# Three small transfers of each head pair's normalisation issued by GpSimd instead of SyncE

## The chip, the cores and the metric

The kernel runs on one core of a Trainium2 chip. The metric is device time in microseconds (us), the median of several runs; lower is better. The engines are PE (TensorE, with PEld for its weight loads), DVE (VectorE), ACT (ScalarE), POOL (GpSimd) and SP (SyncE, which here only issues transfers). Each engine works through its own list of instructions in order.

## What is computed

Attention over 4 batches, 12 heads, 448 positions and a head size of 64, and behind it two feed-forward blocks on 1792 tokens (768 to 2048 to 768, the activation is the square of a relu). All data are float32.

```python
scores = scale * np.matmul(q, k.transpose(0, 1, 3, 2))
scores = cap * np.tanh(scores / cap)
scores = scores - np.max(scores, axis=-1, keepdims=True)
attn = np.exp(scores)
attn = attn / (np.sum(attn, axis=-1, keepdims=True) + 1e-09)
x = np.matmul(attn, v)          # then heads side by side: 1792 x 768
x = (np.maximum(x @ w_in, 0) ** 2) @ w_out      # first block
x = (np.maximum(x @ w_in, 0) ** 2) @ w_out      # second block
```

## The kernel before

Heads are taken two at a time, so a batch has 6 pairs and the kernel has 24. Attention of batch 0 runs first, beside the decoding of weights (`w_early`, `dec`, lines 185 to 211). Then `mlp(b)` (line 246) does the first feed-forward block of batch b on PE, and `weave` (line 711) mixes the attention of batch b+1 into it, piece by piece. The second block (`mlp2`, line 368) comes behind. Each float32 product is made of three matmuls on split operands (`mm`, line 235).

One pair is the generator `att_pair` (line 570): scores and tanh (lines 584 to 594), exp and the product with v (lines 627 to 643), and the normalisation (lines 644 to 690), which this study is about. The normalisation of a pair is a chain of steps, each waiting for the one before:

- The row sums of exp come either out of the matmul itself (pairs called native, line 654 copies them to partition 0 of `sb`) or from two POOL instructions (`partition_all_reduce`, line 610, 10 pairs). They are 2 x 448 numbers on one partition.
- Line 668: a transfer spreads them over 128 partitions (`comp`, 128 x 7). Lines 674 and 675: DVE adds eps and takes the reciprocal.
- Line 676: a transfer writes the 896 numbers to memory (`row`).
- Line 678: two transfers, one for each head, read them back and lay each row over 64 partitions (`rec`, 128 x 448).
- Line 687: DVE multiplies the unnormalised result `u` by `rec`; lines 688 and 689 (ACT, DVE) split it into the two parts of `x`, the input of `mlp(b)`.

The last pair of batch 0 has no such chain, so 23 pairs have one, with four transfers each. Besides these, SP issues every load and store of the kernel: raw weights (line 175, 768 KB each), decoded weights out and in (lines 203 and 183), q, k, v, and results. The order of the instructions on every engine is not the order of the source: the tile framework plans it with a model of the timing (`schedule_with_timeline_sim=True`, line 824), and puts in the semaphore waits. `behind()` (line 147) ties a step's DVE, ACT or SP instructions behind the weight work recorded so far.

Of the kernel before, what the change touches and what calls it, by code (L numbers as in the profile page):

```python
# [17 lines left out]
B, H, S, D = 4, 12, 448, 64  # L18
# [84 lines left out]
def program(ctx: ExitStack, tc, work, capv, sct, eps, qT, kT, v, v1, vl, w_in, w_out, out, guard):  # L103
    nc = tc.nc
# [41 lines left out]
    @contextmanager  # L146
    def behind():

        now, n = dict(marks), len(nc.cur_bb.bb.instructions)
        yield  # L150
        for ins in nc.cur_bb.bb.instructions[n:]:
            if ins.engine in now:
                tc.add_manual_dep(ins, now[ins.engine], mybir.DependencyInfo(
                    mybir.DependencyClass.NoSync, mybir.DependencyReason.DATA), reason="behind the weights")
# [415 lines left out]
    def att_pair(b, pr):  # L570
# [24 lines left out]
        half = [slice(j * D, (j + 1) * D) for j in range(2)]  # L595
        s, sb = work
# [50 lines left out]
        rec = a1.tile([P, S], F32, tag="rec", name="rec")  # L647
        for j in range(2):
# [8 lines left out]
            else:  # L657
                o = a1.tile([P, S], F32, tag="rest", name="rest")
                ACT.activation(o[main], pv[rest], AF.Copy)
                DVE.tensor_tensor(u[main], pv[main], o[main], op=ALU.add)  # L660
        if last:
            DVE.reciprocal(rec, rec)
        else:

            w = 2 * S // P
            comp = a2.tile([P, LINE // 4], F32, tag="comp", name="comp")[:, :w]
            row = dram2.tile([2, S], F32, tag="row", name="row")
            nc.sync.dma_start(out=comp, in_=sb[:1].rearrange("o j s -> o (j s)"))
            yield
            wait = b > 0 and pr < NP - 1  # L670
            if wait:
                yield
            with behind() if wait else ExitStack():
                DVE.tensor_scalar(comp, comp, eps, None, op0=ALU.add)
                DVE.reciprocal(comp, comp)
                nc.sync.dma_start(out=row.rearrange("j s -> (j s)").rearrange("(p w) -> p w", w=w), in_=comp)
                for j in range(2):
                    nc.sync.dma_start(out=rec[half[j]], in_=row[j:j + 1].to_broadcast([D, S]))
            yield
            if wait:  # L680
                yield
                yield
# [9 lines left out]
    def attention(b):  # L692

        live = []
        n = 0
        pr = 0
        while pr < NP or live:
            if pr < NP and n % (LAG0 if b == 0 else LAG) == 0:
                live.append(att_pair(b, pr))
                pr += 1  # L700
            n += 1
            for gen in list(live):
                if next(gen, "end") == "end":
                    live.remove(gen)
            yield
# [125 lines left out]
```

## Time and profile before

| | |
|---|---|
| median of 3 runs | 1117.32 us (1116.66 to 1118.54) |
| the profiled run | 1120.3 us |
| span of its instructions | 1118.5 us |
| PE busy | 1088.4 us (97%) |
| DVE, ACT busy | 865.7 us (77%), 742.3 us (66%) |
| POOL busy | 63.1 us (6%), 24 instructions |
| granted PE clock, mean | 0.993 |

The span reaches from the first to the last instruction; 1.8 us of the profiled run lie around it, and the profiled run is 3.0 us above the median. Times below are microseconds from the start of the span. A busy PE is not PE at its peak, since matmuls are pipelined and their ends are modelled. "Releaser" is what a trace view names as the event that ended a wait; where the named instruction had long been done, another was the real one.

### The profile page before, as it was taken

Reading aid. Unit: us, or ns where it says so; the run is one execution under the profiler, and the core shown is the slowest. Engines: PE = TensorE matmul, PEld = TensorE weight load, DVE = VectorE, ACT = ScalarE, POOL = GpSimd, SP = SyncE. Lnnn points to the kernel's source line nnn. Section 1 sums busy time; section 2 is a strip of 40 time slices with the busy share of each in tenths; the row PEclk is TensorE's granted clock in tenths of the full one; section 3 lists DMA queues with packets and bytes.
Section 4 is the critical chain, followed back from the end, with each engine's and each line's share of the span. In section 5 each row is a group of like instructions: output and inputs, shape, how many; then the busy total and the mean of one; then the engine's idle time right before and its main releaser. Section 6 shows DMA issues by size and latency. Waiting matters only on the chain.

```text
span 1118.5 us, 14514 instructions
## 1 busy us (share of the span) xinstructions
PE 1088.4 (97%) x5088; PEld 948.9 (85%) x5088; DVE 865.7 (77%) x1148; ACT 742.3 (66%) x1036; POOL 63.1 (6%) x24
## 2 busy tenths in 40 slices
PE   6988999989999999999999999999999999999998
PEld 4555989879888799799899999999998999999997
DVE  7778889786989778899778876797789846657663
ACT  6997987657796759998747843565755535555542
POOL 0000002020222021022020000000000000000000
PEclk9998999999999999999999999999999999999999
DMA  8886776855846575756477886885345543333441
GB/s 337 280 297 209 239 241 204 281 160 163 267 139 208 162 258 183 234 189 205 125 246 272 300 291 210 291 301 160 118 134 157 158 136 113 100 112 101 136 126 67
DMA packets 92177, 221.11 MB, mean 198 GB/s; under 512 B 16576, under 2 KB 43072, under 8 KB 92096
## 3 DMA queue, kind: packets, MB, share of 16 engines
q1 hardware_dynamic: 92096, 220.10, 60.2%
q8 instruction: 42, 0.69, 0.2%
q14 instruction: 39, 0.32, 0.1%
HBM read 174.28 MB, written 45.70 MB: 197 GB/s over the span
## 4 chain that ended last, share of the span: by engine, by line
PE 71%; DVE 5%; DMA 4%; ACT 2%; issue 1%; SPq 0%; DVEq 0%; ACTq 0%
PE ps L241 29%; PE st L409 18%; PE st L487 16%; PE pv L641 4%; PE sc L588 3%; DMA rec<-row 1%; DMA scr<-wf 1%; DVE wlo L218 1%; DMA comp<-work 1%; DMA row<-comp 1%; DMA work<-y 0%; DVE wf L194 0%; DVE pl L636 0%; DVE r L193 0%; DVE u L687 0%
## 5 line engine op out<-in xcount | busy, mean ns | idle before, releaser
L218 DVE TENSOR_TENSOR wlo<-wf,whi 128x768 fp32r<-128x768 f32 x240 | 236.9, 989 | 62.6 <-ACT whi L217 62.1
L217 ACT ACTIVATE whi<-wf 128x768 fp32r<-128x768 f32 x240 | 201.1, 839 | 100.0 <-PE st L409 48.4
L241 PE MATMUL ps<-x,whi 128*128 128x448 f32 x768 | 220.6, 368 | 0.0
L241 PE MATMUL ps<-g,whi 128*128 128x448 f32 x768 | 219.9, 367 | 0.0
L409 PE MATMUL st<-xx,whi 128*128 128x448 f32 x672 | 190.9, 367 | 0.0
L487 PE MATMUL st<-t,whi 128*128 128x448 f32 x672 | 187.1, 367 | 0.0
L241 PEld LDWEIGHTS ps<-x,whi 128*128 128x128 f32 x768 | 144.7, 188 | 14.2 <-issue 2.2
L241 PEld LDWEIGHTS ps<-g,whi 128*128 128x128 f32 x768 | 144.4, 188 | 13.7 <-issue 1.8
L241 PE MATMUL ps<-x,wlo 128*128 128x448 f32 x384 | 142.5, 373 | 3.3 <-ACT x L688 3.1
L241 PE MATMUL ps<-g,wlo 128*128 128x448 f32 x384 | 142.1, 371 | 0.0
L487 PEld LDWEIGHTS st<-t,whi 128*128 128x128 f32 x672 | 126.2, 188 | 11.9
L409 PEld LDWEIGHTS st<-xx,whi 128*128 128x128 f32 x672 | 126.2, 188 | 11.3
L409 PE MATMUL st<-xx,wlo 128*128 128x448 f32 x336 | 122.2, 367 | 0.0
L487 PE MATMUL st<-t,wlo 128*128 128x448 f32 x336 | 117.8, 367 | 0.4 <-ACT xx L342 0.4
L593 ACT ACTIVATE t<-sc,sct 128x896 f32<-128x896 f32 x96 | 86.4, 914 | 13.3 <-PE sc L588 12.7
L588 PE MATMUL sc<-ql,kk 128*128 128x448 f32 x192 | 79.9, 416 | 14.1 <-DVE kk L552 8.1
L610 POOL PARTITION_ALL_REDUCE work<-work x20 | 62.9, 3194 | 503.6 <-DVE work L604 293.8
L628 ACT ACTIVATE t<-t,capv 128x896 f32<-128x896 f32 x96 | 89.5, 950 | 0.4
L342 ACT ACTIVATE t<-g 128x896 fp32r<-128x896 f32 x48 | 45.4, 950 | 66.7 <-PE st L487 65.7
L241 PEld LDWEIGHTS ps<-x,wlo 128*128 128x128 f32 x384 | 72.1, 188 | 11.8 <-ACT x L688 4.0
L343 DVE TENSOR_TENSOR t<-g,t 128x896 fp32r<-128x896 f32 x48 | 52.0, 1088 | 37.4 <-ACT t L342 37.4
L241 PEld LDWEIGHTS ps<-g,wlo 128*128 128x128 f32 x384 | 72.1, 188 | 7.5 <-issue 1.6
(102 smaller groups left out, 1508.7 us busy)
## 6 DMA issues: line engine op xcount, KB each, us to landing
wf<-scr SPq DMA_DIRECT2D x215, 384.0 KB, 3.2
raw<-w_in SPq DMA_DIRECT2D x32, 768.0 KB, 5.7
raw<-w_out SPq DMA_DIRECT2D x32, 768.0 KB, 5.9
scr<-wf SPq DMA_DIRECT2D x32, 384.0 KB, 5.4
scr<-wa SPq DMA_DIRECT2D x64, 192.0 KB, 4.3
scr<-ss SPq DMA_DIRECT2D x48, 192.0 KB, 4.2
q_r<-qT SPq DMA_DIRECT2D x18, 448.0 KB, 4.6
k_r<-kT SPq DMA_DIRECT2D x18, 448.0 KB, 4.0
```

The source lines that it names most:

```text
L217: mark(ACT.activation(hi, f, AF.Copy))
L218: mark(DVE.tensor_tensor(lo, f, f32(hi), op=ALU.subtract))
L241: PE.matmul(ps, lhsT=w[:, i, :], rhs=x[part][:, j, :], start=first and n == 0, stop=last and n == len(terms) - 1)
L342: ACT.activation(hi, t, AF.Copy)
L343: DVE.tensor_tensor(lo, t, f32(hi), op=ALU.subtract)
L409: PE.matmul(ps, lhsT=w[:, i + c, :], rhs=x[:, kk_, c, :], start=first and c == 0 and n == 0, stop=c == 2 and n == 2, skip_group_check=not ...
L487: PE.matmul(banks[b][e], lhsT=w[:, 3 * f + e, :], rhs=x[:, f, :], start=first and q == f == n == 0, stop=q == 3 and f == 1 and n == 2, ski ...
L588: PE.matmul(sc[:, 0 if shared else j, :S], lhsT=kchunk(kk, j, c), rhs=q[:, j, :], start=n == 0 if shared else n % 2 == 0, stop=n == 3 if s ...
L593: ACT.activation(t[c], sc[:, 0, :S] if shared else sc[:, :, :S], AF.Tanh, scale=sct)
L610: POOL.partition_all_reduce(out[:, j], s[:, j], P, op)
L628: ACT.activation(t[c], t[c], AF.Exp, scale=capv)
L641: PE.matmul(pvs[j], lhsT=vv[:, j, c, :], rhs=m_ if c == KC else m_[:, j, :], start=c == 0 and m_ is moving[0], stop=c == KC and m_ is movi ...
```

## The change

All four transfers of the chain move from SP's list to POOL's. What they move, and what waits for them, stays as it was.

```diff
-            nc.sync.dma_start(out=comp, in_=sb[:1].rearrange("o j s -> o (j s)"))
+            nc.gpsimd.dma_start(out=comp, in_=sb[:1].rearrange("o j s -> o (j s)"))
...
-                nc.sync.dma_start(out=row.rearrange("j s -> (j s)").rearrange("(p w) -> p w", w=w), in_=comp)
+                nc.gpsimd.dma_start(out=row.rearrange("j s -> (j s)").rearrange("(p w) -> p w", w=w), in_=comp)
                 for j in range(2):
-                    nc.sync.dma_start(out=rec[half[j]], in_=row[j:j + 1].to_broadcast([D, S]))
+                    nc.gpsimd.dma_start(out=rec[half[j]], in_=row[j:j + 1].to_broadcast([D, S]))
```

## Rows read from the trace of the kernel before

**Rows 1.** The page, part 1: engine, busy us (share), instructions.

```profile
PE 1088.4 (97%) x5088; PEld 948.9 (85%) x5088; DVE 865.7 (77%) x1148; ACT 742.3 (66%) x1036; POOL 63.1 (6%) x24
```

**Rows 2.** Windows: stretch, length, busy us (count) by engine, PE clock, DMA share, GB/s.

```profile
56.00:84.00 28.00, 22.82 (x78) 14.15 (x76) 21.82 (x36) 26.81 (x36) 0.00 (x0) 0.94 0.90 296
84.00:100.00 16.00, 11.96 (x38) 7.79 (x38) 15.81 (x20) 10.60 (x15) 0.00 (x0) 0.79 0.65 220
```

**Rows 3.** Timeline of PE, 56 to 92: start, us, instruction [idle before, releaser].

```profile
83.44 0.68 PE L241 MATMUL ps<-x,wlo 128*128 128x448 f32 x2 [3.14 <-ACT x L688]
88.15 0.71 PE L588 MATMUL sc<-ql,kk 128*128 128x448 f32 x1 [4.04 <-DVE ql L553]
```

**Rows 4.** Waits of DVE, 28 to 100: us in total, times, longest us.

```profile
DVE u L687 <- DMA rec<-row: 4.8, 3, 3.0
```

**Rows 5.** Timeline of DVE, 28 to 112.

```profile
82.15 0.62 DVE L687 TENSOR_TENSOR u<-u,rec 128x448 f32<-128x448 f32 x1 [3.03 <-DMA rec<-row]
```

**Rows 6.** Issue to landing of lines 668, 676, 678, in that order, 28 to 100.

```profile
DMA to landing us min/median/max: 4.4/6.1/8.2
...
DMA to landing us min/median/max: 4.0/4.7/6.7
...
DMA to landing us min/median/max: 2.7/3.3/6.0
```

**Rows 7.** The same three landings for pair 3 of batch 0 alone, 62 to 77.

```profile
DMA to landing us min/median/max: 5.5/5.5/5.5
...
DMA to landing us min/median/max: 6.1/6.1/6.1
...
DMA to landing us min/median/max: 5.7/5.8/6.0
```

**Rows 8.** The same lines, 100 to 600: SP's issue (ns min/median/max), then landing.

```profile
L668 SPq DMA_DIRECT2D comp<-work x18: 497/501/1112, 101.3 to 569.7; - x18
DMA to landing us min/median/max: 2.1/3.3/6.1
...
L676 SPq DMA_DIRECT2D row<-comp x18: 319/320/424, 124.2 to 572.6; - x18
DMA to landing us min/median/max: 1.4/2.6/6.6
...
L678 SPq DMA_DIRECT2D rec<-row x36: 450/532/1601, 127.2 to 576.5; - x36
DMA to landing us min/median/max: 2.7/3.0/7.1
```

**Rows 9.** Lines 610 and 194, all their instructions: ns min/median/max, first and last.

```profile
L610 POOL PARTITION_ALL_REDUCE work<-work x20: 2951/3246/3318, 173.2 to 564.0; - x20
...
L194 DVE SCALAR_TENSOR_TENSOR wf<-wf,r x32: 919/957/2600, 19.7 to 235.9; 128x768 int32<-128x768 int32 x32
```

**Rows 10.** Waits of PE, whole span.

```profile
PE pv L641 <- DVE pl L636: 4.6, 3, 3.0
```

**Rows 11.** Waits of SP's list, whole span.

```profile
SPq L678 <- DMA row<-comp: 48.1, 23, 4.7
```

**Rows 12.** Chain that ended last, 240 to 262: start, us, what.

```profile
251.38 6.95 DMA rec<-row
```

**Rows 13.** Timeline at the ends of attention of batches 1, 2 and 3.

```profile
259.11 0.58 ACT L688 ACTIVATE x<-u 128x448 fp32r<-128x448 f32 x1 [6.27 <-DVE u L687]
...
259.74 0.47 PE L241 MATMUL ps<-x,wlo 128*128 128x448 f32 x1
...
421.99 0.58 ACT L688 ACTIVATE x<-u 128x448 fp32r<-128x448 f32 x1 [4.95 <-DVE u L687]
...
423.29 0.36 PE L241 MATMUL ps<-x,wlo 128*128 128x448 f32 x1
...
580.30 0.58 ACT L688 ACTIVATE x<-u 128x448 fp32r<-128x448 f32 x1 [4.36 <-DVE u L687]
...
585.23 0.36 PE L241 MATMUL ps<-x,wlo 128*128 128x448 f32 x1
```

## Prediction

> **What bounds the kernel now.** The page comes first: PE is busy for 1088.4 of 1118.5 us [rows 1], so 30 us at most can be won by feeding PE better, whatever is done to transfers. The second view is the table of windows, which says where PE is not full. Between 56 and 100 us, the end of batch 0's attention, PE idles 9.2 us (28 - 22.82 and 16 - 11.96), and its granted clock falls to 0.94 and 0.79, that is, part of the stretch at the lower of its two levels [rows 2]. The third view, PE's timeline, gives the two largest gaps: 3.14 and 4.04 us [rows 3]. The first names ACT's step on x, which stands behind the product with `rec`. In the second half of that stretch DVE is busy 15.81 of 16 us [rows 2]: there DVE sets the pace, and PE's gaps are DVE's delays. The fourth view, DVE's waits, shows what delays it: 4.8 us for `rec`, three times [rows 4], 3.03 us of it in one wait that ends at 82.15 [rows 5]. So in batch 0 the normalisation chain stands on the path, and there alone by much. Later PE is nearly full, and the chain touches the end at one point per batch: the last pair's x, which `mlp(b)` needs for its sixth chunk.
>
> **What is moved.** 23 pairs x 4 transfers = 92 issues leave SP and come to POOL, which has 20 instructions in the program proper [rows 9]. Nothing is added and nothing computed differently. The waits go along: SP stood 48.1 us, 23 times, for `row` to land before it could issue line 678 [rows 11]; now POOL stands there.
>
> *SP relieved.* What was queued behind SP's 48.1 us are loads and stores of weights. The waits that stand out on DVE in batch 0 and on PE later are for `rec` and `pl` [rows 4, 10], not for weights, so I count this at nothing; if that cover were gone, the bound is 2.1 us (48.1 / 23) for each load that was late.
>
> *POOL's queue.* Behind a POOL transfer waits the next pair's all-reduce, and behind the two all-reduces of a pair (2 x 3.25 = 6.5 us [rows 9]) waits an earlier pair's transfer if the planner orders it so. A chain would then be 6.5 us later; behind batch 0 PE's longest waits are for `pl` and not for x [rows 10], so outside the three stage ends I take nothing.
>
> *Issue on POOL.* No POOL issue stands in the trace. Bounds: SP's own for the same transfers, 0.50 + 0.32 + 0.53 + 0.53 = 1.9 us per chain [rows 8], and POOL's one kind of real work, 3.25 us an instruction [rows 9], so 13.0 us per chain. It can't be below SP's by more than that 1.9 us. I take 1.0 us an issue, twice SP's row, because the transfers are the same and an all-reduce reads and writes whole tiles: 4.0 us a chain, +2.1 us. The Trainium skill (DMA: Bandwidth & Descriptors, SWDGE vs HWDGE vs iDMA) says that GpSimd makes the descriptors in software and is slower to the first byte, about 1 us against 0.6; by that the sum would be +0.4 us on each of three hops, and no run here shows it yet.
>
> *Queueing.* On SP a transfer of 3.5 KB stands behind 768 KB weight loads issued just before it. The medians from issue to landing in batch 0 are 6.1, 4.7 and 3.3 us, 14.1 together [rows 6]; the smallest seen later are 2.1, 1.4 and 2.7, 6.2 together [rows 8]. So about 8 us of a chain in batch 0 is queueing; pair 3, the one behind the 3.03 us wait, took 5.5, 6.1 and 5.8 [rows 7], 17.4 us, or 11.2 over the smallest. A list of POOL's own may pass all of SP's backlog or none of it. I take half, because the same DMA engines are 0.90 busy in that stretch [rows 2]: -5.6 us for pair 3, and with the dearer issue -5.6 + 2.1 = -3.5 us.
>
> Here a page speaks for and against. The Trainium skill (DMA: Bandwidth & Descriptors, Queues, rings and completion order) says that an engine goes round between the queues that have work, packet by packet, by which nearly the whole -11.2 us would come. The same page (Issuing engines are not separate DMA queues) says that transfers issued by several engines run on the same 16 and that only issue time is saved, by which nothing of it would come: that is the second rival below.
>
> *Batch 0.* 3.5 us earlier covers the 3.03 us wait; the two smaller ones would go too, 4.8 us in all [rows 4]. Only what is not absorbed by a later DVE wait counts. Behind the 3.03 us DVE runs full (15.81 of 16 [rows 2]), so that one counts whole: -3.0 us, between 0 (the next wait, for loads, takes it) and -4.8.
>
> *Later batches.* Medians are 3.3 + 2.6 + 3.0 = 8.9 us against 6.2 [rows 8]; half of 2.7 is -1.3, with issue +2.1 it is +0.8 us a chain, hidden wherever x is early. At the three stage ends the room is: batch 1, 259.11 + 0.58 = 259.69 against PE's 259.74, 0.05 us; batch 2, 422.57 against 423.29, 0.7 us; batch 3, 580.88 against 585.23, 4.35 us [rows 13]. In batch 1 the last hop took 6.95 us [rows 12], 4.25 over the smallest; half of that, 2.1, pays the dearer issue. I take 0 for all three, with +0.8 at batches 1 and 2 (+0.9 together beyond the room) as the near bound and the first rival as the far one.
>
> *DVE beside POOL.* Beside an all-reduce a DVE instruction of 0.96 us took up to 2.60 [rows 9], and PE lost 4.6 us in three gaps to that kind of delay [rows 10]: 0.23 us per all-reduce. If an issue hurt DVE in proportion to its length, 92 x 0.23 x 1.0 / 3.25 = 6.5 us. It can't be a gain, since POOL only gets more work. I take 0, because a transfer's issue does not read tiles, and keep +6.5 as the bound. The Trainium skill (SBUF — State Buffer, Who interferes with whom) has the clash the other way round too: DVE instructions that take both ports lock GpSimd out, and descriptors wait; by the 0.96 us of a DVE instruction here [rows 9] that would be under 1 us an issue.
>
> *The plan.* The order of all engines is planned with modelled times, so 92 moved issues can shift neighbours. The price of such a shift is that of the single gaps that such delays leave now, 0.5 to 3 us [rows 10], either way.
>
> **Sum.** Against the profiled run, 1120.3 us: -3.0 + 0 + 0 = 1117.3 us; that run was 3.0 above the median, so the median comes to 1114.3 us.
>
> **The rivals**, all on the median, 1117.3 us.
>
> 1. *Longer hops show at the stage ends (slower).* Place: PE's sixth chunk at 259.7 and 423.3. Price of an issue i: the chain grows by 4i - 1.9 - 2.1 there, and batch 0's gain is 5.6 + 1.9 - 4i = 7.5 - 4i while it is under 3.0. Loss (beyond 0.05 and 0.7 us of room) and gain meet at i = 1.4 us; from there on it is slower. At i = 2.0 the chain grows 4.0: 3.95 + 3.3 = 7.25 us of gaps and nothing gained in batch 0. Gaps of that size now (3.14 + 4.04) go with a clock of 0.79 over 16 us [rows 2, 3], another 3.4 us: 1117.3 + 10.6 = 1127.9 us. For it: all-reduces of 3.25 us show POOL's software as slow. Against: the work per issue is small. Chance 0.14.
> 2. *The queue is not left behind (slower, less).* The backlog sits in the shared DMA engines, and the chain only gets +2.1 us of issue: the 3.03 us wait grows by 2.1, batch 1 loses 2.05, batch 2 1.4, together +5.6: 1122.9 us. For it: the engines are 0.90 busy in batch 0 and 0.65 behind it [rows 2]. Against: line 676 moves the same 3.5 KB in 1.4 to 6.7 us [rows 6, 8] with what SP issued just before. Chance 0.14. The Trainium skill's second sentence above is this rival.
> 3. *Hidden anyway (no change).* The 3.03 us reappear as a wait for a load or for ACT, which is busy 26.81 of 28 us from 56 to 84 [rows 2]; or the gain is paid back at batches 1 and 2. 1117.3 us. Chance 0.28.
>
> **How the numbers follow.** The forecast, 1114.3 us, has 0.44. A measurement of this kernel tells about 0.2% (2.2 us) from no change; faster by more is below 1115.1. The range goes from 1110.5 (-4.8 instead of -3.0, and 2 us of the plan) to 1124.0, which takes in the second rival and the DVE bound beside the gain (-3.0 + 6.5) and leaves the far rival out. Chances: faster 0.44, same 0.28, slower 0.28.
>
> **What would show it.** Right: in batch 0 the landings of the three lines fall well under 6.1, 4.7 and 3.3 us, DVE's wait of 3 us for `rec` near 80 us is gone, and mlp's first matmuls and all later stage ends stand about 3 us earlier. Wrong: POOL's issues take over 1.4 us; the landings stay; PE waits for x at 260 and 423 us grow; or new DVE instructions of 2 us stand beside POOL's issues.

## The result and the profile after

| | before | after | ratio, 95% interval |
|---|---|---|---|
| first measurement, median (us) | 1117.06 (n 4) | 1126.95 (n 4) | 1.0085 [1.0068, 1.0103] |
| repeated, median (us) | 1119.73 (n 35) | 1123.15 (n 12) | 1.0032 [1.0011, 1.0053] |

The change makes the kernel slower, by 0.3 to 0.9%; the two intervals do not overlap, so its size is known no closer than that. The prediction was faster by 0.3%. The first measurement lies outside its range (1110.5 to 1124.0), the repeated one inside it, but both moved the other way. In the profiled execution of after the span is 1123.9 us, against 1118.5.

The page of after, part 1 (as [rows 1]), and the list in part 3 that is new:

```profile
PE 1089.4 (97%) x5088; PEld 947.4 (84%) x5088; DVE 863.4 (77%) x1148; ACT 742.4 (66%) x1036; POOL 113.9 (10%) x116
...
q0 software_dynamic: 3680, 5.45, 1.9%
```

POOL has its 92 transfers. DVE's busy time is not larger than before. So neither is the loss DVE being slowed beside POOL's issues, nor did PE get more to do.

Windows of after (as [rows 2]):

```profile
56.00:84.00 28.00, 22.26 (x77) 13.10 (x76) 24.54 (x38) 27.30 (x38) 6.07 (x11) 0.96 0.90 305
84.00:100.00 16.00, 11.98 (x32) 7.37 (x33) 13.87 (x16) 10.01 (x13) 1.04 (x2) 0.71 0.83 276
```

PE idles as much at the end of batch 0 as before (5.7 and 4.0 us), at a lower granted clock in the second stretch (0.71 against 0.79). Nothing was gained in the place where all of the forecast gain was to be. DVE's waits for `rec` there, 28 to 100 us (as [rows 4]), and the two waits of PE for x (as [rows 3]):

```profile
DVE u L687 <- DMA rec<-row: 3.1, 2, 2.2
```

```profile
80.06 0.67 PE L241 MATMUL ps<-x,wlo 128*128 128x448 f32 x2 [1.60 <-ACT x L688]
...
94.48 0.68 PE L241 MATMUL ps<-x,wlo 128*128 128x448 f32 x2 [2.35 <-ACT x L688]
```

Issue and landing of lines 668, 676 and 678 in after, first 28 to 100 us (as [rows 6]), then 100 to 600 us (as [rows 8]); the landing line belongs to the issue line above it:

```profile
L668 POOL DMA_DIRECT2D comp<-work x4: 544/547/573, 44.4 to 72.4; - x4
...
DMA to landing us min/median/max: 5.0/5.8/6.1
L676 POOL DMA_DIRECT2D row<-comp x5: 545/577/581, 44.9 to 81.0; - x5
...
DMA to landing us min/median/max: 4.6/6.0/6.8
L678 POOL DMA_DIRECT2D rec<-row x10: 516/530/602, 49.8 to 87.4; - x10
...
DMA to landing us min/median/max: 3.9/5.5/7.2
...
L668 POOL DMA_DIRECT2D comp<-work x18: 547/564/590, 108.1 to 570.7; - x18
...
DMA to landing us min/median/max: 2.0/3.0/5.9
L676 POOL DMA_DIRECT2D row<-comp x18: 540/542/577, 130.9 to 575.4; - x18
...
DMA to landing us min/median/max: 1.7/3.0/6.2
L678 POOL DMA_DIRECT2D rec<-row x36: 516/530/595, 134.1 to 581.1; - x36
...
DMA to landing us min/median/max: 2.7/4.5/7.0
```

Here is the surprise. One issue takes 0.53 to 0.58 us, about as long as SyncE's. But no backlog was left behind: in batch 0 the three medians are 17.3 us together, where before had 14.1, and later `rec` lands in 4.5 us instead of 3.0 with the same smallest value, 2.7. For pair 3 of batch 0 alone, the pair of [rows 7], the three landings in after are these:

```profile
DMA to landing us min/median/max: 6.0/6.0/6.0
...
DMA to landing us min/median/max: 6.8/6.8/6.8
...
DMA to landing us min/median/max: 5.3/6.1/6.8
```

The chain of waits (the critical chain of each trace) shows a second price. First after, then before, at comparable chains, from DVE's reciprocal to the issue of line 678 (start, us, what):

```profile
228.69 0.12 DVE comp L675
228.81 0.44 issue
229.25 1.72 DMA row<-comp
230.97 0.02 issue
231.00 0.04 POOLq L678
231.04 0.51 issue
231.55 0.53 POOL rec L678
```

```profile
223.54 0.21 DVE comp L675
223.76 1.81 DMA row<-comp
225.59 0.02 SPq L678
225.63 0.45 SPq L678
```

SyncE begins its issue 0.02 us after `row` has landed, GpSimd 0.58 us after (medians over all 23 chains), and 0.41 instead of 0.03 us behind DVE's reciprocal. From the reciprocal to the landing of both halves of `rec`, the median of the 18 chains behind batch 0 is 6.5 us in before and 9.8 us in after. By the medians of the hops 2.9 of these 3.3 us are 0.4 in front of line 676, 0.4 more for `row`, 0.56 in front of line 678, and 1.5 more for `rec`.

DVE's waits for `rec` over the whole span (us, times, longest), in after:

```profile
DVE u L687 <- DMA rec<-row: 34.8, 13, 5.4
```

In before they were 28.3 us. That is far less growth than 18 chains longer by 3.3 us would give. Which of this is the transfers and which is the new order that the planner made was the first question.

### The profile page after: what moved, and what is told of

Its sections match the earlier page's. It is cut to its first block, busy times and chain, and to the rows that moved or that the text cites. A ratio compares the mean times of both kernels' runs of the same rounds, so it can differ in the third digit from the quotient of the medians.

```text
span 1123.9 us, 14522 instructions
## 1 busy us (share of the span) xinstructions
PE 1089.4 (97%) x5088; PEld 947.4 (84%) x5088; DVE 863.4 (77%) x1148; ACT 742.4 (66%) x1036; POOL 113.9 (10%) x116
## 3 DMA queue, kind: packets, MB, share of 16 engines
q0 software_dynamic: 3680, 5.45, 1.9%
## 4 chain that ended last, share of the span: by engine, by line
PE 70%; DVE 5%; ACT 2%; issue 2%; DMA 1%; POOL 0%; DVEq 0%; POOLq 0%; ACTq 0%
PE ps L241 29%; PE st L409 18%; PE st L487 16%; PE pv L641 4%; PE sc L588 3%; DVE wlo L218 1%; DVE pl L636 1%; DMA scr<-wf 0%; ACT t L593 0%; ACT whi L217 0%; DVE wf L194 0%; ACT t L628 0%; DMA out<-o 0%; DMA rec<-row 0%; DVE r L193 0%
## 5 line engine op out<-in xcount | busy, mean ns | idle before, releaser
L241 PEld LDWEIGHTS ps<-g,whi 128*128 128x128 f32 x768 | 144.2, 188 | 14.1 <-issue 1.7
L241 PEld LDWEIGHTS ps<-x,wlo 128*128 128x128 f32 x384 | 72.1, 188 | 14.1 <-ACT x L688 5.7
```

Source lines behind the costliest of these rows:

```text
L241: PE.matmul(ps, lhsT=w[:, i, :], rhs=x[part][:, j, :], start=first and n == 0, stop=last and n == len(terms) - 1)
```

## The experiments

**The order and the issuer, apart.** The program is built twice. The first build records the planned order of PE, DVE, ACT and SyncE, the second is tied to it; GpSimd's own list is planned anew. So one kernel has the order of before with GpSimd as issuer, and the other the order of after with SyncE. In the traces the four engines do stand in that order, instruction for instruction, the moved transfers left out. (The change also takes lines 676 and 678 out of SyncE's share in `behind()`, which ties nothing on GpSimd's list; with the order held this moves nothing else.)

```diff
+    PLAN, RUN = 'sync', 'gpsimd'     # pool_oldplan;  sync_newplan: 'gpsimd', 'sync'
+    mine = [by_place[n] for n in places if by_place[n].engine.name == engine]
+    for a, b in zip(mine, mine[1:]):
+        tc.add_manual_dep(b, a.name, ...)
```

> POOL issues the four transfers, but PE, DVE, ACT and SP keep instruction for instruction the order of the kernel before (the program is planned once with SP as the issuer, and that order is then imposed). If the loss of 9.9 us comes from the new plan: 1117 us within 2 us. If it comes from what POOL's transfers cost on the chip (row and rec land in 4.3 and 4.6 us instead of 3.0 and 3.0): about 1127 us, with DVE's waits for rec grown beyond the 28.3 us of before. Half and half: about 1122 us.

> The mirror image: SP issues the four transfers as before, but PE, DVE, ACT and SP stand in the order of the changed kernel. If the new plan is the cause: about 1127 us, with the block of 16 native pv matmuls of 8.4 us near 98 us and DVE idle from 100 to 112 us. If POOL's transfers are the cause: about 1117 us.

Measured: 1138.21 us, ratio 1.0166 [1.0113, 1.0219], for GpSimd in the order of before; 1121.03 us, ratio 1.0000 [0.9979, 1.0022], for SyncE in the order of after. So no cost of the new order can be told, within 0.2% either way, and with the order of before the issuer costs twice to five times what the change as a whole does, more than any of the three times that were expected (1117, 1122, 1127 us). DVE's waits for `rec` say how both go together. GpSimd in the order of before:

```profile
DVE u L687 <- DMA rec<-row: 58.1, 16, 10.4
```

SyncE in the order of after:

```profile
DVE u L687 <- DMA rec<-row: 15.4, 6, 6.4
```

With SyncE the order of after has 13 us fewer waits than that of before (15.4 against 28.3): it puts the product with `rec` later behind its transfers. Counted in these two traces over the 23 chains, DVE has 159 us of other work between its reciprocal and the product in the order of after, and 118 us in that of before. With GpSimd the waits grow by 30 us in the order of before (58.1 against 28.3) and by 19 us in the order of after (34.8 against 15.4). So the new order covers more of the longer hops, and in time 0.3 to 0.9% is left of a price of 1.7%.

One thing stays open here. In the one trace of each, both kernels with the order of after reach PE's 300th matmul some 4 us later than before (84 to 112 us: 67 and 69 matmuls, 82 in before), while the medians show no price of that order.

**One part alone, each with a plan of its own.** Batch 0 only, the later batches only, line 678 only, and lines 668 and 676 only; before and after were repeated beside the last two. Each ratio is to the executions of before in the same set (median 1122.02 us for the first two kernels, 1119.73 for the others).

```diff
+            q = nc.gpsimd if b == 0 else nc.sync      # b0_only;  b13_only: b > 0
-            nc.sync.dma_start(out=comp, ...)
+            q.dma_start(out=comp, ...)
...
-                    nc.sync.dma_start(out=rec[half[j]], ...)
+                    nc.gpsimd.dma_start(out=rec[half[j]], ...)   # rec_only: this line alone
```

> POOL issues for batch 0 alone (5 pairs), SP for batches 1 to 3, planned anew. In the changed trace PE is 5.2 us behind the kernel before at its 275th matmul (107 us) and 4.1 us behind at the end, so if the loss sits in batch 0: 1122 to 1127 us. If it sits in the later stages: 1117 us.

> POOL issues for batches 1 to 3 alone (18 pairs), SP for batch 0, planned anew. If the loss sits in batch 0: 1115 to 1117 us (from 107 us to the end the changed trace gains 1.1 us on the one of before). If each POOL transfer costs: about 1125 us.

> Only line 678 (two transfers of 112 KB a pair) is issued by POOL; comp and row stay with SP. rec is the hop that got longer in the changed trace (median 3.0 to 4.5 us from 100 to 600 us, 3.3 to 5.5 in batch 0). If that hop is the cost: most of the loss is here, ratio 1.004 to 1.006. If the loss is in the new plan whatever is moved: it can be anywhere between 0.998 and 1.006, with the rec landings no guide to it.

> Lines 668 and 676 (3.5 KB each) are issued by POOL, line 678 stays with SP. Their landings hardly moved in the changed trace (3.0 and 3.0 us against 3.3 and 2.6). If only the rec hop costs: no change, ratio within 0.2% of 1. If any transfer on POOL costs: 1.003 or more.

> The kernel before once more, as the measure of what differs between executions of one and the same program. In its first trace 2193 of PE's back-to-back matmuls stand 0.2067 us apart and 1986 stand 0.2027 us apart, in long stretches; if the slower spacing comes and goes by itself, other stretches have it here, the total moves by up to 9 us, and the span without that excess stays near 1109.6 us.

> The changed kernel on the same chip and beside the same runs as the experiments. Taken without the excess of the slower matmul spacing, its first trace is 6.7 us longer than that of before (1116.3 against 1109.6). If that is what the change costs: ratio near 1.006. If the 9.9 us of the first measurement are all of the change: 1.009. If the first pair of measurements differed by chance: 1.000.

| moved | median (us) | ratio, 95% interval |
|---|---|---|
| batch 0 only | 1121.94 | 1.0003 [0.9983, 1.0023] |
| batches 1 to 3 only | 1118.74 | 0.9992 [0.9962, 1.0021] |
| line 678 only | 1121.58 | 1.0013 [0.9991, 1.0035] |
| lines 668 and 676 only | 1119.03 | 0.9995 [0.9969, 1.0020] |
| nothing | 1117.93 | 0.9999 [0.9973, 1.0026] |
| all | 1123.15 | 1.0032 [1.0011, 1.0053] |

With its own plan no part alone can be told from no change; only all of it can. For line 678 alone 1.004 to 1.006 had been expected if its hop is the cost: its landings did grow (median 3.9 us from 100 us on), but DVE waits 30.9 us for `rec`, hardly more than the 28.3 of before. No part is faster either, batch 0 with its 3.03 us wait included. These kernels mix the hop with a new order each time, so the cause had to be looked for with the order held.

**Does SyncE's wait shelter `rec`?** When SyncE issued line 678, it stood until `row` had landed [rows 11] and issued no bulk transfer meanwhile. I counted over the 36 transfers of line 678 behind batch 0 how many others had been issued and landed over 0.5 us later: on the average 0.6 in before, 2.2 in after. So the wait itself might be what keeps the engines empty. The next kernel makes SyncE stand at both places again, with the order of before; another does so with the plan of the changed kernel.

```diff
+                nc.sync.dma_start(out=hold, in_=comp[:1, :1])   # four bytes
                 nc.gpsimd.dma_start(out=row..., in_=comp)
+                nc.sync.dma_start(out=hold, in_=row[:1, :1])    # four bytes
                 for j in range(2):
                     nc.gpsimd.dma_start(out=rec[half[j]], ...)
```

> The same kernel as in the earlier run with the order of before and GpSimd as issuer (1138.21 us, ratio 1.0166): the yardstick for the next kernel on the same chip. Both theories: ratio to before 1.011 to 1.022; rec lands in 3.9 us (median behind 100 us), with 1.9 other transfers in flight on the average when it is issued, against 0.6 in before.

> GpSimd issues as in the kernel beside it and every engine keeps the order of before, but SyncE reads four bytes of comp and four bytes of row at the two places where it used to issue lines 676 and 678, so that it stands for the same two events as before (48.1 us for row and 32.9 us for comp in before) and issues no bulk transfer meanwhile. Theory A (SyncE's wait had kept the DMA engines empty for the next hop; the move took that shelter away): transfers in flight at rec's issue fall from 1.9 to about 0.6, rec's median behind 100 us from 3.9 to 3.0 to 3.2 us, row's from 2.9 to about 2.6, and the time comes back to 1117 to 1123 us, ratio to before 0.998 to 1.005. Theory B (GpSimd's issue or its list is slower by itself, whatever SyncE does): rec stays at 3.8 to 4.5 us and the ratio at 1.012 or more. In between: both have a part, in proportion.

> The changed kernel, with its own plan, and SyncE reading four bytes of comp before GpSimd issues line 676 and four bytes of row before line 678. Theory A: rec's median behind 100 us falls from 4.5 to 3.0 to 3.4 us, and the time to that of the kernel in which SyncE issued in the changed kernel's order (ratio 1.0000), that is 0.998 to 1.002. Theory B: rec stays at 4.3 us or more and the ratio at 1.003 to 1.0085, as the changed kernel's two measurements had it.

Measured, against the same runs of before: 1.0150 [1.0117, 1.0182] without the reads, 1.0230 [1.0194, 1.0266] with them, and 1.0110 [1.0072, 1.0147] for the changed kernel with them. SyncE did stand, as its waits in pool_oldplan_hold show (line 845 is the read of four bytes), yet `rec` landed as late as without (the same kernel, 100 to 620 us):

```profile
SPq L845 <- DMA row<-comp: 62.1, 22, 5.1
```

```profile
DMA to landing us min/median/max: 2.7/4.2/6.8
```

So theory A falls: SyncE standing until `row` lands does not bring `rec` back. `row`'s landing now releases both lists at once, and what counts is what follows. One chain, issued by SyncE and GpSimd after a landing at 501.40 us:

```profile
501.42 0.56 SPq L845 DMA_DIRECT2D hold<-row  x1
501.70 1.11 POOL L680 DMA_DIRECT2D rec<-row  x2 [1.44 <-DMA row<-comp]
502.07 0.34 SPq L183 DMA_DIRECT2D wf<-scr  x1
```

GpSimd's first half of `rec` is issued 0.56 us behind the landing, SyncE's next bulk transfer 0.67 us and GpSimd's second half 1.13 us (medians of the 23 chains). So the first half is ahead in all 23, mostly by 0.1 to 0.4 us, and the second is behind a bulk transfer in 17. In before SyncE issues both halves and its next transfer stands 1.2 us behind the first. A lead that short did not help (`rec`'s median stays 4.2 us), a longer one did: in the three chains behind batch 0 in which the next bulk transfer came 1.0 to 2.5 us behind GpSimd's first half, both halves landed in 2.7 to 3.2 us, as from SyncE. (How many transfers were in flight can't be told in this kernel: the landings of SyncE's transfers aren't in its trace.) Theory B, that GpSimd's issue is slower by itself, expects these landings too; the next experiment sets it apart.

The reads also suggest that SyncE relieved was worth something: with them the kernel is 0.8 points slower in the order of before (1.0230 against 1.0150). In the changed kernel, planned anew, 1.0110 can't be told from the first 1.0085, only from 1.0032. How much of it the 46 extra small transfers cost by themselves wasn't measured, so the gain is not shown.

**The hop by itself.** Behind the end of the kernel, line 676 and the two transfers of line 678 are repeated three times in six settings, each gated by DVE, in one execution. Theory C is that `rec` needs its place ahead of the bulk transfers.

```diff
+                if v in ("Sbehind", "Plater"):
+                    bulk()                      # three loads of 384 KB by SyncE
+                small()                         # by GpSimd for names with P, else by SyncE
+                if v in ("Sahead", "Pbeside"):
+                    bulk()
```

> The kernel before with a measurement behind its end, when the engines are idle: line 676 and the two transfers of line 678 three times each in six settings, every one gated by DVE and finished before the next. Salone and Palone: SyncE or GpSimd issues them and nothing else runs. Sahead: SyncE issues them and three loads of 384 KB behind them in the same list. Pbeside: GpSimd issues them while SyncE issues the three loads at the same event. Sbehind: SyncE issues the three loads first. Plater: SyncE issues the three loads some 1.5 us earlier than GpSimd the small ones. The time is longer by the added work and says nothing. Theory C (place in the list): rec's landing is 2.6 to 3.0 us in Salone, Palone and Sahead (at most 0.5 more), and 1 to 4 us more in Pbeside and Plater; Sbehind is the dearest of SyncE's. Theory B (GpSimd's issue by itself): Palone lands 1 to 1.5 us behind Salone, and Pbeside no more than 0.4 us behind Palone.

DVE's waits there, 1100 to 1361 us (us in total, times, longest):

```profile
DVE whi L839 <- DMA recPbeside<-prow: 19.3, 3, 6.6
...
DVE whi L839 <- DMA recSbehind<-prow: 18.2, 3, 6.1
DVE whi L839 <- DMA recPlater<-prow: 15.6, 3, 5.9
DVE whi L839 <- DMA recPalone<-prow: 11.1, 3, 3.8
...
DVE whi L839 <- DMA recSahead<-prow: 10.9, 3, 3.9
DVE whi L839 <- DMA recSalone<-prow: 8.9, 3, 3.5
```

The first of the three with SyncE alone is no measure: the kernel was still at its last products, and DVE did other work in the wait, so that it shows 1.97 us. The next one is clean:

```profile
1110.95 0.62 DVE L473 TENSOR_TENSOR u<-st,u 128x448 f32<-128x448 f32 x1 [0.39 <-PE st L487]
1113.54 0.16 DVE L839 TENSOR_TENSOR whi<-whi,recSalone 128x4 f32<-128x4 f32 x1 [1.97 <-DMA recSalone<-prow]
...
1197.66 0.16 DVE L839 TENSOR_TENSOR whi<-whi,recSalone 128x4 f32<-128x4 f32 x1 [3.38 <-DMA recSalone<-prow]
```

Without it, SyncE's hop alone is 3.4 to 3.5 us, and GpSimd's 3.7 (11.1 by thirds), so issuing from GpSimd costs 0.2 to 0.3 us by itself. In front of three bulk loads in its own list SyncE's hop is 3.6 us. GpSimd's, beside the same three loads, is 6.4 us, no better than SyncE's behind them, 6.1; with the loads some 1.5 us earlier it is 5.2. From issue to landing the same transfers from GpSimd take these times, alone and beside the loads:

```profile
recPalone<-prow POOLq DMA_DIRECT2D x6, 112.0 KB, 2.7
...
recPbeside<-prow POOLq DMA_DIRECT2D x6, 112.0 KB, 5.3
```

That is theory C with a small part of B: of the 2.8 us between GpSimd beside the loads and SyncE ahead of them (6.4 - 3.6), 0.2 to 0.3 is the issuer alone and about 2.5 the place. "Beside" turns out to be mostly behind: the same DVE instruction gates both lists, but SyncE issues two of the three loads before GpSimd's first transfer (at 1148.98 and 1149.39 against 1149.66 us). The packets in the trace show where the time goes. Alone, GpSimd's first packet starts 1.2 us after its issue (SyncE's too) and the last 1.5 to 1.7 us later; beside the loads the first starts after 2.5 to 2.6 us and the last 2.8 to 3.0 us later. So about half of what is lost is lost before the first packet. No run issued them from ScalarE, so the runs do not tell whether any second list would lose this place or only GpSimd's. The 3.5 KB of line 676 behave the same way: from GpSimd 1.7 to 1.8 us to landing alone and 4.3 to 4.4 beside the loads, from SyncE 1.4 both alone and ahead of them (one landing of each is on record).

It also fits what stands in the kernel. In before 20 of the 36 transfers of line 678 found nothing in flight, had others issued behind them within 2.5 us, and landed in 2.98 us on the average. In after only 4 of 36 were so placed, and these too landed in 2.98 us; the other 32 took 4.5 us on the average.

**Which hop carries it.** The order of before is kept once more, and line 678 alone, or lines 668 and 676 alone, go to GpSimd.

```diff
-                    nc.sync.dma_start(out=rec[half[j]], ...)     # rec_oldplan
+                    nc.gpsimd.dma_start(out=rec[half[j]], ...)
...
-            nc.sync.dma_start(out=comp, ...)                     # comprow_oldplan, with row
+            nc.gpsimd.dma_start(out=comp, ...)
```

> GpSimd issues line 678 alone; all other transfers stay with SyncE, and every engine keeps the order of before. All four moved in this order cost 1.015 to 1.017. Theory C: rec is the hop that had empty engines and loses them, so it carries most: ratio 1.007 to 1.016, rec's median behind 100 us at 3.7 us or more. If instead the cost is spread over the hops, or comes from GpSimd's own list (a transfer waits there behind another pair's), the ratio is 1.005 or less.

> GpSimd issues lines 668 and 676, SyncE line 678, and every engine keeps the order of before. Theory C: comp and row stood behind bulk transfers in SyncE's list already and lose little (row by 0.5 us), rec stays first in its list at 3.0 to 3.4 us: ratio 1.000 to 1.006. If the cost comes from GpSimd's list or is spread, 1.007 to 1.012.

Measured: 1.0158 [1.0112, 1.0204] for line 678 alone, 1.0017 [0.9992, 1.0041] for the other two. DVE's waits for `rec`, first with line 678 moved, then with the other two:

```profile
DVE u L687 <- DMA rec<-row: 54.1, 18, 9.6
```

```profile
DVE u L687 <- DMA rec<-row: 32.9, 17, 6.3
```

Line 678 alone costs all that the four cost (1.0150 and 1.0166), so it is not the two small hops. Nor is it GpSimd's list: with line 678 moved each issue begins 0.3 to 0.8 us behind `row`'s landing, so nothing stands in front, and the all-reduces do not come late behind GpSimd's waits (the first of each pair starts 0.1 to 0.2 us behind DVE's last sum, as in before). In this kernel `rec`'s median behind batch 0 is 4.1 us, with 1.7 other transfers in flight at its issue (counted as above); with the other two moved it stays at 3.0, with 0.6.

One hop did gain, by a term that counts neither as issue nor as landing. SyncE issues line 668 on the average 1.7 us after its data are there, because it stands elsewhere in its list; GpSimd does so after 0.4 to 0.5 us. DVE's waits for `comp`, in before and with lines 668 and 676 moved:

```profile
DVE comp L674 <- DMA comp<-work: 17.1, 11, 3.2
```

```profile
DVE comp L674 <- DMA comp<-work: 5.9, 6, 1.6
```

That may be why 1.0017 can stand beside a chain from the reciprocal to `rec` that is no shorter there than with line 678 moved (medians 7.8 and 7.5 us, 6.5 in before). Line 668 by itself was not run, and the waits do not add up to the time in every kernel: with all four moved DVE waits 13 us less for `comp` than with line 678 alone (4.0 against 17.5 us), at the same price.

On PE, 13.8 of the 18.1 us by which the trace with line 678 moved is longer than that of before are idle time (1136.6 - 1092.7 = 43.9 against 30.1), and 4.3 us are busy time, at a mean granted clock of 0.991 instead of 0.993. Part of the idle time stands at the end of batch 0. In front of the product with `ql` it is 4.04 us in [rows 3] and 5.75 us in the second trace of before, 4.99 us with line 678 moved, and 6.42 and 7.40 us in the two traces with all four moved, the last in pool_oldplan_again:

```profile
94.67 0.71 PE L588 MATMUL sc<-ql,kk 128*128 128x448 f32 x1 [7.40 <-DVE ql L553]
```

## Why the prediction was wrong

**The step that failed is Queueing, "I take half".** It took 14.1 us of landings as 6.2 us of transfer and 8 us of standing behind SyncE's backlog, of which a list of its own would pass half: -5.6 us for pair 3 (half of 17.4 - 6.2). Measured for pair 3 in after: 6.0, 6.8, and 5.3 and 6.8 us, against 5.5, 6.1 and 5.7 and 6.0 [rows 7]: instead of 5.6 us shorter, the three are some 1.5 us longer. The three medians of batch 0 rose by 3.2 us. The time behind bulk transfers is spent in the shared engines, not in SyncE's list (6.4 us beside three loads from GpSimd, 6.1 behind them from SyncE), so another list does not save it. And the step read a list as something to stand behind only. For `rec` it was a place at the front: SyncE issued it first when `row` landed, and everything later stood 1.2 us behind it. The row for that was there: line 678's median was 3.0 us with a smallest of 2.7 [rows 8], a hop with next to no queueing, of which half could not be had. Adding up three lines hid that the last one had only something to lose. What a list does hold back is the issue itself: the 1.7 us that line 668 waited for SyncE's turn, which the step did not count, since it measured from the issue on.

**Of the two page sentences, the one that spoke against it held.** The Trainium skill (DMA: Bandwidth & Descriptors, Issuing engines are not separate DMA queues) says that issuers share the engines and only issue time is saved; the probe agrees, 6.4 us beside the loads from GpSimd and 6.1 behind them from SyncE. That engines go round between lists packet by packet (Queues, rings and completion order) is not disproved by these runs, but it does not bring the small transfer through early: 2.7 us alone, 5.3 beside three loads, with the first packet 1.3 us later.

**Issue on POOL.** The duration was sized too large (1.0 us taken, 0.53 to 0.58 measured) and a term was missing: the 0.4 and 0.56 us between the released wait and the issue, where SyncE has 0.02 to 0.03. By both the chain gets 0.3 us from durations (0.55 + 0.58 + 2 x 0.53 = 2.2 against 1.9) and about 0.9 us from starts, so the +2.1 us had the right sign and the wrong make-up.

**Batch 0.** DVE's waits for `rec` in 28 to 100 us fell only from 4.8 to 3.1 us, with a longest of 2.2, and PE's idle time in 56 to 100 did not fall (9.2 and 9.8 us): the -3.0 us never came. The kernel with batch 0 alone (1.0003) says the same.

**Later batches.** Taken as +0.8 us a chain and hidden, measured +3.3. Half of it or more is indeed hidden, since the plan moved; with the order of before all four cost 1.5 to 1.7%. The half of 2.7 us that was to come back did not: `row` and `rec` landed later, and `comp` 0.3 us earlier.

**Rival 1 (stage ends)** did not happen in after. PE waits for ACT's x twice in the whole span of after, 3.9 us, both times in batch 0 (80.06 and 94.48 us); nothing stands at 260 or 423 us. With the order of before and line 678 moved it shows in small: PE waits 0.98 us for x at 265.83 and 1.28 us at 598.06. **Rival 2 (the queue is not left behind)** came nearest: its 1122.9 us stands beside 1123.15 to 1126.95. Its mechanism, the backlog in the shared engines, is what the runs show; but its price was issue time at stage ends, and the real one is `rec`'s lost place, paid by DVE all along attention. That the two times are close is luck. **Rival 3** is what moving one part alone gives.

**What held.** DVE beside POOL at 0: DVE is busy 863.4 us against 865.7 [rows 1], and line 194's longest on `wf` is the same (2.60 us); its 2.80 us on `wa` at 286.45 us stands beside an all-reduce, not a transfer. The plan within 0.5 to 3 us: 1.0000 with 2.4 us of interval. POOL's queue at 0: lines 668 and 676 alone cost 1.0017. Twice in after a transfer did stand behind a pair's all-reduces (4.0 us at line 678 near 493 us, 5.5 at line 676 near 518 us), and DVE waited for `rec` in neither chain. "SP relieved" at 0 is open: the kernels with the four-byte reads point to a gain, smaller than the loss at `rec`.

## What to carry to other kernels

Before a transfer is moved to another list, look at what it had in the old one: here the one that landed near its smallest time stood first and lost by the move, and the one that gained was the one whose issue waited for its turn after its data were there. Read the landing and the wait before the issue apart: the first was not shortened by another list, the second was. An issuer that waits in order for a small transfer and then issues the next one gives that next one a lead over its bulk transfers; time spent in that wait is not only loss. And let the order be kept in one of the experiments: the planner's new order hid half or more of a price that was 1.5 to 1.7% by itself, and made the cost of each part look like nothing.

## What the runs showed of the hardware

GpSimd's issue begins 0.41 us after the DVE instruction that releases it and 0.56 to 0.58 us after a landing (medians), SyncE's 0.02 to 0.03 us after either. From the issue to the first packet of line 678 both take 1.2 us on idle engines (the probe). The 112 KB of line 678 go as fewer packets from GpSimd: with that line alone moved, its 46 transfers are 2208 packets on GpSimd's list and 3680 fewer on SyncE's.

Executions of one kernel differ by up to 1% with nothing changed (before ran 1114.4 to 1125.9 us in one set), and part of it is PE's pace at an unchanged granted clock. From 900 to 1000 us PE is busy for 100.00 us at clock 1.00 in two executions of the kernel before, first in the first trace, then in the repeated one:

```profile
900.00:1000.00 100.00, 100.00 (x485) 90.84 (x484) 58.18 (x75) 50.12 (x58) 0.00 (x0) 1.00 0.38 118
```

```profile
900.00:1000.00 100.00, 100.00 (x495) 92.66 (x495) 59.16 (x77) 51.84 (x59) 0.00 (x0) 1.00 0.39 119
```

That is 2% between 485 and 495 matmuls, over long stretches in either pace. Taken without the excess of the slower spacing, which is an estimate from the starts of the matmuls, the two traces of before differ by about 1 us instead of 4.2 (spans 1118.5 and 1114.3). A comparison of two single traces carries this, which is why the verdicts above rest on repeated times and on landings. What sets the pace was not found.
